# Moving the fold of row-group partial sums ahead in the first batch, and storing the last block in halves

One core of one Trainium2 chip runs the whole program. The metric is device time in microseconds (us), the median over runs; the span that a run's trace shows is some 1.8 us shorter. "Faster" or "slower" means a difference of over 2%.

## The reference, cut to what matters

```python
# x: (4, 12416, 128), inducing: (32, 128)
def mab(q, kv):
    s = scale * (q @ kv.transpose(0, 2, 1))
    a = np.exp(s - s.max(-1, keepdims=True))
    a /= a.sum(-1, keepdims=True) + 1e-09
    return a @ kv

h = mab(I, x)                 # 32 x 128 per batch: a sum over all 12416 rows
y = mab(x, h)                 # then every row of x attends to h
gate = 1 / (1 + np.exp(-(y @ w_gate)))          # 128 -> 1536
out  = (gate * (y @ w_val)) @ w_out             # 1536 -> 128
```

For the first batch, h has to be complete before anything of the large second part can begin. That stretch, from the last piece of x to the first tanh (the sigmoid is computed as a tanh), is called the head below. The part after it, the body, is the gate, value and output matmuls of all four batches. The tail is the last block's eviction and store.

## The kernel before: the parts that matter

The program is a list of named operations with their dependencies, and a recorded order of names for each engine. The order is what is played; names such as `fill8.2` are filler matmuls, eight of them here, that only keep TensorE busy.

```python
ACC = ps("acc", [P, TOK])                       # one PSUM tile for the sums of the first batch
hsum, hval = ACC[:, 288:320], ACC[:, 256:288]

def h_base():                                   # the fold: partial sums of row groups -> hval, hsum
    hev = dve(129, fin, "hev", ... tensor_copy(out=hacc, in_=ACC[:, 0 : P + 1]))
    sbc = dve(32, [hev], "hb0", ... tensor_scalar_mul(out=ssb, in0=I4, scalar1=hacc[:, P : P + 1]))
    ...                                         # "hbase": two fp32 matmuls on PE

def stage1_first(i, groups, xts):               # quad i: scores, exp, sums
    apart = i < NQ - 1                          # NQ = 6: quads 0..4 by row groups, quad 5 in place
    ...
    if apart:   # 4 row groups at once, into ACC[r:r+32, 0:129]
    else:       # in place: ones16 -> hsum, x -> hval
    fin.append(a)                               # "hv{i}.{k0}"

def h_first():
    r = dve(256, fin, "hr0", ... reciprocal(out=hden, in_=hsum))
    hTd[0] = dve(32, [r], "hc0", ... tensor_tensor(out=hT, in0=hval, in1=hden, op=ALU.mult))

def fill(o, n):
    for _ in range(n):
        PE.matmul(ACC[:, 320:512], lhsT=ident, rhs=zeros, start=False, stop=False, ...)

# last step of a unit of 4 row blocks
e = act(nt * P, ..., ACT.activation(out=os.t[:, 0:nt, :], in_=ACC[:, 0 : nt * P], func=AF.Copy, scale=0.5))
st = op("SP", ..., SP.dma_start(ov[b][:, 4 * u : 4 * u + nt, :], os.t[:, 0:nt, :]))
```

The recorded order of PE around the end of the head:

```
... hv2.0 hv3.0 fill10.1 xt4.0 ... xt5.13 s1t5.8 s1t5.0 hbase s1t5.13 hv5.8 hv5.0 hv5.13 s2t0 fo0.1 s2t2 fo0.0 sb0.2 ...
```

`xt` are transposes of x, `s1t` the scores of h, `hv` its sums, `s2t` the scores of the second attention, `fo` the folds of h into the value and gate weights.

The softmax here doesn't subtract the row's maximum and nothing guards it: scores larger than these inputs give would overflow.

## Time and profile before

| | before |
|---|---|
| time, three runs | 698.72, 699.49, 698.71 us |
| span of the profiled run | 697.2 us |
| ACT busy | 675.3 us (97%) |
| reciprocal of the sums (start) | 24.07 us |
| last cast of wv on POOL (start, length) | 24.30, 0.61 us |
| first tanh | 27.67 us |
| last eviction to end of span | 693.31 to 697.18: 3.87 us |

ACT (ScalarE) bounds the body, so only a head that ends earlier or a shorter tail can shorten the run. The prediction shows the lines.

### The profile page before, as it was taken

The numbers are of one execution on the slowest core, as the hardware profiler recorded it, in microseconds if no ns is written. First come the engines' busy times: TensorE is split into PE (matmuls) and PEld (weight loads), VectorE is DVE, ScalarE is ACT, GpSimd is POOL, SyncE is SP. The second block draws the span as 40 slices with busy tenths as digits, with TensorE's granted clock in tenths as the row PEclk, the third lists the DMA queues.
The fourth block names the chain that finished last, engine by engine and source line by source line (L and its number), as shares of the span: only waits on it lengthen the run. The fifth ranks groups of instructions, "written<-read, shape, count | busy, mean of one in ns | idle before, by whom it ended". The sixth has DMA issues, their size and how long they took to land.

```text
span 697.2 us, 20697 instructions
## 1 busy us (share of the span) xinstructions
PE 672.5 (96%) x8325; PEld 384.6 (55%) x8325; DVE 667.4 (96%) x1130; ACT 675.3 (97%) x867; POOL 435.8 (63%) x498
## 2 busy tenths in 40 slices
PE   7899999999999999999999999999999999999997
PEld 5545555555555555555555555555555555555555
DVE  4799999999999999999999999999999999999997
ACT  4899999999999999999999999999999999999995
POOL 4446756855739657766485575775674675667664
PEclk9999999999999999999999999999999999999999
DMA  9859796693655646746556559422333222242211
GB/s 352 190 127 184 162 176 157 134 184 85 146 129 135 133 109 156 149 117 140 107 123 155 122 106 140 141 71 87 88 113 109 56 85 99 63 131 89 83 48 50
DMA packets 121874, 87.72 MB, mean 126 GB/s; under 512 B 80913, under 2 KB 105009, under 8 KB 121777
## 3 DMA queue, kind: packets, MB, share of 16 engines
q1 hardware_dynamic: 117584, 76.44, 43.1%
q0 software_dynamic: 4144, 9.93, 9.2%
q8 instruction: 65, 1.06, 0.6%
q14 instruction: 33, 0.26, 0.1%
q10 hardware_dynamic: 48, 0.02, 0.0%
HBM read 39.99 MB, written 38.01 MB: 112 GB/s over the span
## 4 chain that ended last, share of the span: by engine, by line
PE 51%; ACT 26%; DVE 12%; issue 5%; DMA 3%; POOL 2%; SPq 0%; ACTq 0%; DVEq 0%; POOLq 0%
PE acc L635 26%; ACT tga L635 20%; PE v L635 17%; DVE ua L635 12%; PE g L635 8%; ACT vs L635 3%; ACT os L635 3%; DMA ua<-in_x_dram 2%; DMA xT<-in_x_dram 1%; DMA out_dram<-os 1%; POOL sm L635 0%; SPq L635 0%; POOL ua L635 0%; POOL pt L635 0%; ACT e L635 0%
## 5 line engine op out<-in xcount | busy, mean ns | idle before, releaser
L635 DVE SCALAR_TENSOR_TENSOR ua<-tga,v 128x512 f16<-128x512 f16 x1041 | 641.4, 682 | 10.6 <-PE v L635 3.0
L635 ACT ACTIVATE tga<-g 128x1024 f16<-128x1024 f32 x576 | 569.0, 1142 | 0.6 <-PE g L635 0.4
L635 PE MATMUL acc<-wo,ua 128*128 128x128 f16 x4608 | 358.8, 220 | 3.2 <-ACT os L635 0.2
L635 PEld LDWEIGHTS <-ua 128*128 128x128 f16 x4608 | 262.4, 98 | 169.2 <-issue 160.4
L635 PE MATMUL v<-a2r,hw 32*128 32x512 f16 x1200 | 322.3, 374 | 8.6 <-DVE ua L635 4.3
L635 POOL TENSOR_TENSOR pt<-tga,vs 128x512 f32<-128x512 f16 x111 | 129.1, 1163 | 171.4 <-ACT vs L635 73.6
L635 PE MATMUL g<-a2r,hw 32*128 32x512 f16 (+1 forms) x1200 | 225.7, 376 | 3.5 <-ACT tga L635 1.9
L635 PEld LDWEIGHTS <-hw 32*128 32x128 f16 x2400 | 88.7, 91 | 110.1 <-issue 44.0
L635 POOL TENSOR_TENSOR ua<-pt,vs 128x512 f16<-128x512 f32 x111 | 140.9, 1269 | 9.9 <-issue 1.2
L635 ACT COPY vs<-v 128x512 f32<-128x512 f32 x111 | 77.6, 701 | 0.2 <-PE v L635 0.2
L635 ACT ACTIVATE os<-acc 128x512 f32<-128x512 f32 (+1 forms) x99 | 68.9, 696 | 2.5 <-PE acc L635 2.4
L635 POOL TENSOR_TENSOR sm<-sm,minus 128x16 f32<-128x16 f32 (+1 forms) x21 | 63.9, 3043 | 1.6
L635 POOL TENSOR_TENSOR a2n<-e2t,sm 128x128 f16<-128x128 f16 x96 | 37.2, 482 | 1.3 <-DVE sm L635 0.4
L635 POOL DMA_DIRECT2D x<-in_x_dram x18 | 11.2, 621 | 41.5 <-ACT tga L635 40.1
L635 POOL TENSOR_TENSOR tree<-tree 128x64 f32<-128x64 f32 (+4 forms) x69 | 23.7, 343 | 5.4
L635 POOL TENSOR_TENSOR tree<-e2t 128x256 f32<-128x256 f16 (+1 forms) x23 | 15.8, 688 | 8.3 <-DMA e2t<-e 8.3
L635 ACT ACTIVATE e<-g 128x512 f16<-128x512 f32 (+1 forms) x23 | 17.0, 737 | 0.1
L635 DVE COPY xT<-g 128x1024 f16<-128x1024 f16 (+1 forms) x12 | 8.0, 666 | 8.5 <-PE g L635 8.5
L635 ACT ACTIVATE eT<-g 128x512 f16<-128x512 f32 (+1 forms) x18 | 13.0, 721 | 0.0
L635 PE MATMUL g<-ident,x 128*128 128x128 f16 x97 | 7.6, 220 | 2.7 <-ACT x L635 1.3
L635 PE MATMUL g<-xT,hT 128*32 128x512 f16 (+1 forms) x108 | 9.4, 363 | 0.0
L635 DVE SCALAR_TENSOR_TENSOR ut<-tgt,v 128x512 f16<-128x512 f16 (+1 forms) x16 | 8.7, 550 | 0.3 <-PE v L635 0.2
(83 smaller groups left out, 153.7 us busy)
## 6 DMA issues: line engine op xcount, KB each, us to landing
out_dram<-os SPq DMA_DIRECT2D x96, 256.0 KB, 2.5
a2r<-dr SPq DMA_DIRECT2D x23, 512.0 KB, 4.6
dr<-a2p SPq DMA_DIRECT2D x19, 512.0 KB, 3.5
x<-in_x_dram POOLq DMA_DIRECT2D x15, 512.0 KB, 5.6
xT<-in_x_dram SPq DMA_DIRECT2D x6, 512.0 KB, 7.4
dr<-a2p SPq DMA_DIRECT2D x4, 640.0 KB, 3.3
x<-in_x_dram POOLq DMA_DIRECT2D x3, 544.0 KB, 7.8
ua<-in_x_dram SPq DMA_DIRECT2D x3, 512.0 KB, 11.5
```

Of the source, the lines that this page charges most:

```text
L635: ins = fn(*a, **k)
```

## The change

Its intent: fold the partial sums of quads 0 to 3 while the core still waits for loads, and sum quads 4 and 5 in place, so that no fold stands between the last piece of x and h; and store the last block in two halves, so that the first half's bytes leave while the second half is evicted.

```diff
-            apart = i < NQ - 1
+            apart = i < NQ - 2
...
-    h_base()                       # after quads 0..4
+        if i == NQ - 3:            # after quads 0..3
+            h_base()
...
-        e = act(nt * P, ..., f"E{b}.{u}", ...)
-        st = op("SP", ..., SP.dma_start(ov[b][:, 4 * u : 4 * u + nt, :], os.t[:, 0:nt, :]))
+        for k in range(2 if (b, u) == (B - 1, NB - 1) else 1):
+            lo, hi = ...           # two blocks each for the last unit
+            e = act((hi - lo) * P, ..., f"E{x}{b}.{u}", ...)
+            q, n = (ACT, "ACT") if k else (SP, "SP")
+            st = op(n, ..., q.dma_start(ov[b][:, 4 * u + lo : 4 * u + hi, :], os.t[:, lo:hi, :]))
```

The recorded orders were made anew. The pieces that count:

```diff
 PE
-  ... hv2.0 hv3.0 fill10.1 xt4.0 ... xt5.13 s1t5.8 s1t5.0 hbase s1t5.13 hv5.8 hv5.0 hv5.13 s2t0 fo0.1 s2t2 fo0.0 sb0.2
+  ... s1t4.0 fill8.1 xt4.8 hbase xt5.0 ... s1t5.13 hv5.0 hv5.8 hv5.13 fill8.2 s2t0 s2t2 fo0.1 fo0.0 fill3.7 sb0.2
 ACT
-  ... xs2t0 fc0.1 xs2t2 fc0.0 ...             ... E3.22 E3.24 E3.23
+  ... xs2t0 xs2t2 fc0.1 fc0.0 ...             ... E3.22 E3.24 E3.23 Eh3.23 sth3.23
```

## The prediction

> **What bounds the kernel now.** I read the page first (busy time of the engines), then the busy time by stretches, then the timeline of the first 30 us and of the last 14 us, because the change touches only those two ends.
>
> ```profile
> PE 672.5 (96%) x8325; PEld 384.6 (55%) x8325; DVE 667.4 (96%) x1130; ACT 675.3 (97%) x867; POOL 435.8 (63%) x498
> ...
> 5.00:10.00 5.00, 4.10 (x58) 2.81 (x57) 2.15 (x4) 2.65 (x4) 2.03 (x3) 1.00 1.03 418
> 15.00:20.00 5.00, 4.11 (x95) 3.48 (x92) 2.07 (x3) 2.80 (x6) 2.01 (x4) 1.00 1.03 401
> 25.00:30.00 5.00, 4.88 (x108) 2.59 (x105) 4.32 (x14) 4.98 (x10) 0.56 (x1) 1.00 0.58 88
> ```
>
> The last three lines are stretches; their columns are the length, then busy time of PE, its weight loads, DVE, ACT and POOL, the clock, the DMA share and GB/s. Until 20 us the loads run at 400 to 418 GB/s with a DMA share of 1.03 and every engine has gaps: the prologue is bound by the loads of x. From 25 us ACT is full. Summed over the five stretches of 0 to 25 us ACT is busy 12.2 us, over 680 to 697.2 us 9.1 us; so from 25 to 680 us it is busy 675.3 - 21.3 = 654.0 of 655 us. The body is ACT's, without slack. Whatever makes ACT begin its unbroken run earlier is kept to the end, and nothing else before 25 us counts.
>
> So the head is the way from the last piece of x (landed by 20.2 us) to the first tanh at 27.67 us. The timeline, cut to what matters (start, length, engine, operation):
>
> ```profile
> 20.16 0.29 DVE L635 CAST x<-ua 128x256 f16<-128x256 f32 x1 [0.35 <-DMA ua<-in_x_dram]
> ...
> 21.54 0.29 DVE L635 COPY hacc<-acc 128x129 f32<-128x129 f32 x1 [0.48 <-PE acc L635]
> 21.95 0.58 DVE L635 TENSOR_SCALAR ssb<-I,hacc 128x32 f32<-128x32 f32 x1
> 22.45 0.41 DVE L635 COPY xT<-g 128x512 f16<-128x512 f16 x1
> 22.59 0.41 PE L635 MATMUL acc<-ssb,ones 128*128 128x32 f32 x2
> 24.07 0.36 DVE L635 RECIPROCAL hden<-acc 128x32 f32<-128x32 f32 x1 [1.21 <-PE acc L635]
> 24.30 0.61 POOL L635 CAST wv<-tga 128x512 f16<-128x512 f32 x1
> 24.46 0.19 DVE L635 TENSOR_TENSOR hT<-acc,hden 128x32 f16<-128x32 f32 x1
> 24.97 0.29 PE L635 MATMUL g<-wv,hT 128*32 128x256 f16 x2
> 25.30 0.37 ACT L635 CAST hw<-g 128x256 f16<-128x256 f32 x1
> 26.19 0.41 PE L635 MATMUL v<-ident,nb 128*32 128x128 f16 x16
> ```
>
> The fold of the partial sums (copy of the accumulator, scaled identity, two pairs of fp32 matmuls) stands between the last transposes and h: the scaled identity holds DVE up to 22.45, when the last xT copy starts, and the ssb matmuls hold PE up to 22.92. h comes out at 24.46 + 0.19 = 24.65. Note the POOL line: the last weight cast ends at 24.91, and the first fold matmul on wv starts at 24.97. The weights are ready only just after h.
>
> The tail is one path with no overlap:
>
> ```profile
> 693.31 0.60 ACT L635 ACTIVATE os<-acc 128x512 f32<-128x512 f32 x1 [2.42 <-PE acc L635]
> 693.93 0.33 SPq L635 DMA_DIRECT2D out_dram<-os  x1
> ...
> 694.70:694.80 0.10, 0.00 (x0) 0.00 (x0) 0.00 (x0) 0.00 (x0) 0.00 (x0) 1.00 0.39 143
> 695.40:695.50 0.10, 0.00 (x0) 0.00 (x0) 0.00 (x0) 0.00 (x0) 0.00 (x0) 0.50 0.51 185
> ```
>
> Bytes flow from about 694.75 to 695.5, 0.8 us after the issue; then come the receipt and the closing waits, to 697.2.
>
> **What the skill says.** The Trainium skill, "DMA: Bandwidth & Descriptors", section "Anatomy of one DMA", gives about 2.0 us fixed plus bytes over 436 GB/s, most of the fixed part being the receipt after the last byte (fitted there on the GpSimd path). The trace half agrees: stores of 256 KB land in 2.2 us at the end, about 0.75 us of it data. Halving a transfer saves only data time. Its section "Issuing engines are not separate DMA queues" says a second issuing engine saves only issue time: the same here, the two halves share 16 DMA engines. "Perfetto Trace Analysis", section "Optimizing Scalar/DVE Operations", gives every ScalarE operation a fixed access overhead: the trace has 0.60 us for 128x512 and 0.37 us for 128x256 from PSUM, so 0.14 fixed and 0.23 per 256 columns. "TensorEngine Tiling (Array Packing)", "Key Properties", says that a change of tiling mode drains the array; quad 4 loses two such changes, too small for me to see in the timeline.
>
> **The change part by part.**
>
> *Fold earlier.* Quads 0 to 3 still accumulate by row groups; their fold now comes behind the ninth xT copy (the first of quad 4), in time in which DVE and PE wait for loads (DVE busy 2.07 of 5 us in 15 to 20). It is the same work: copy 0.29, scaling 0.58, PE about 0.7. Quad 4 is now summed in place: for each group of 8 blocks 16 matmuls, 0.40 us (23.29 to 23.69 for such a group), where 8 by row groups took 0.30: +0.2 us on PE for both groups. I walked the new PE order with these durations: xt4.8 at 18.7, fold matmuls to 19.85, xt5.0 and xt5.8 to 20.6, s1t4.8 and hv4.0 to 21.25, xt5.13 to 21.5, then s1t5.0, s1t5.8, hv4.8, s1t5.13, and the three last sums to about 23.4. The reciprocal then starts near 23.5 instead of 24.07: h comes about 0.55 us earlier (an estimate from these rows).
>
> *What of it is kept.* Not 0.55. Loads and POOL's order are untouched, so the last weight cast still ends near 24.91 and the fold on wv still starts at 24.97; the copy hw at 25.30 does not move, nor does the score matmul behind it, which needs the PSUM buffer that this copy frees at 25.67 (it starts at 25.72). What moves: the second row group (s2t2) goes ahead of the fold, so its 0.35 us on ACT falls into idle time. And nb is ready at about 25.6 instead of 26.13, so the transposes at 26.19 can start when the score matmul lets them, at about 25.95. From there the path to the first gate matmul is as before (copy 26.65 becomes 26.41, ends 26.83, gate 27.24 becomes 27.00). ACT: 25.30 + 0.29 + 0.49 + 0.49 + 0.27 + 0.49 = 27.32, plus some 0.1 of gaps. Both say first tanh at 27.42 to 27.43 against 27.67: a gain of **0.24 us**, which ACT carries through the body. The order of the body is the same except for the renumbered fills.
>
> *Halves of the last store.* Both halves wait for the last matmul (the second has no wait of its own). First half: 693.31 + 0.37, issued by SP near 693.70, 0.23 earlier. Second: starts 0.27 later, ends 693.95 (0.04 later than the whole one), issued by ACT. It moves 128 KB, 0.4 us less of data, the first half being nearly through by then. 0.40 - 0.04 - about 0.08 for the issue on ACT (0.42 us there at the start of the kernel against 0.33 on SP) = **0.28 us**.
>
> Sum: 0.24 + 0.28 = 0.52; 698.72 - 0.52 = **698.2 us**.
>
> **Rivals.** (a) The weights do not bind and h's whole 0.55 us is kept: for it, wg is cast well ahead and only wv's second part is late; against it, 24.91 and 24.97 in the trace and an unchanged POOL order. Time: 697.9. (b) The head gives nothing, because ACT's work from 25.30 on is packed and the new order of PE (16 more matmuls in quad 4, xt5.13 behind hv4.0) takes the slack back: 698.45. (c) The second half's store costs as much as it saves, since ACT's queue has issued nothing since the first microsecond and two receipts must now arrive: tail 0, time 698.5. (d) A different phase makes the body collect waits, say on PSUM buffers: ACT idles only about 1 us in 655 now, so a new order of arrivals can only lose; 0.5 us lost would return the time to 698.7.
>
> **Range and chances.** The runs of before spread from 698.71 to 699.49, as much as the whole gain. Rivals (a) with a full tail and (b) with (c) span 697.9 to 698.7; with the run-to-run spread I take 697.3 to 699.0. Two per cent are 14 us, and both ends together hold under 12 us beyond the loads: the verdict "same" is nearly certain.
>
> **What would show it.** Right: hacc and ssb before 19 us; reciprocal of hden near 23.5; the wv fold and hw still at 24.97 and 25.30; eb 128x256 before hw; first tanh near 27.4; ACT full from there; two os of 128x256 at the end, stores from SP and ACT, bytes over by about 695.2 less the head's gain. Wrong: a wv cast that ends elsewhere than 24.9; a first tanh at 27.1 (rival a) or 27.6 (b); a last byte no earlier after the last matmul than 2.2 us (c); ACT idle in the body up by more than 0.2 us (d).

## The result, and the profile after

Runs of the changed kernel: 699.25, 699.29, 699.46, 700.42 us, median 699.38; of the kernel before on the same chip: 698.71, 698.72, 699.39, 699.49, median 699.06. A ratio here is the mean time of one kernel's fast runs over that of the other's fast runs of the same rounds, so it is not quite the ratio of those medians: 1.0008, with a 95% interval of 0.999 to 1.0025. The time, 699.38, lies above the predicted range (697.3 to 699.0). Where 0.5 us were to be won, none was.

The page's busy line first (busy time, share of the span, number of instructions):

```profile
PE 675.1 (97%) x8350; PEld 386.9 (55%) x8350; DVE 666.7 (95%) x1130; ACT 675.5 (97%) x868; POOL 435.8 (62%) x498
```

PE has 25 more matmuls. Sixteen come from quad 4, summed in place (two per block of rows instead of one); the other nine can only be fillers. Next, two of the stretches that were shown of before, with the same columns:

```profile
15.00:20.00 5.00, 4.63 (x117) 4.04 (x114) 2.95 (x6) 3.78 (x10) 2.33 (x4) 1.00 1.03 401
...
25.00:30.00 5.00, 4.33 (x71) 2.11 (x69) 3.26 (x12) 3.06 (x8) 0.56 (x1) 0.67 0.31 39
```

Before 20 us DVE and ACT do more, as planned. From 25 to 30 us ACT is busy 3.06 of 5 us where it was full before, and the granted clock is 0.67. The timeline of the changed kernel's head (start, length, engine, operation, idle time before it and what ended it):

```profile
17.74 0.28 DVE L636 COPY hacc<-acc 128x129 f32<-128x129 f32 x1
...
18.15 0.24 DVE L636 TENSOR_SCALAR ssb<-I,hacc 128x32 f32<-128x32 f32 x1
...
22.90 0.25 PE L636 MATMUL acc<-ae,x 128*128 128x32 f16 x4
23.00 0.33 PE L636 MATMUL acc<-zeros,ident 128*128 128x192 f16 x2
24.23 0.61 POOL L636 CAST wv<-tga 128x512 f16<-128x512 f32 x1
24.43 0.66 PE L636 MATMUL acc<-zeros,ident 128*128 128x192 f16 x6 [1.10 <-issue]
25.12 0.36 DVE L636 RECIPROCAL hden<-acc 128x32 f32<-128x32 f32 x1 [3.25 <-PE acc L636]
25.51 0.19 DVE L636 TENSOR_TENSOR hT<-acc,hden 128x32 f16<-128x32 f32 x1
...
29.75 7.44 ACT L636 ACTIVATE tga<-g 128x1024 f16<-128x1024 f32 x8 [0.20 <-PE g L636]
```

The fold is early (17.74 and 18.15, both before 19 us as predicted), and the sums are done at 23.15 instead of 24.05. But the reciprocal starts at 25.12, not near 23.5. It waits for `acc`, and what still writes `acc` are eight filler matmuls, in front of which PE even stood idle for 1.10 us with nothing awaited. The first tanh starts at 29.75, which is 2.08 us later than before. The tail, as timeline and bytes (last two columns of the short stretches: DMA share and GB/s):

```profile
695.00 0.66 ACT L636 ACTIVATE os<-acc 128x256 f32<-128x256 f32 x2 [2.42 <-PE acc L636]
695.69 0.38 ACTq L636 DMA_DIRECT2D out_dram<-os  x1
```

```profile
696.20:696.30 0.10, 0.00 (x0) 0.00 (x0) 0.00 (x0) 0.00 (x0) 0.00 (x0) 1.00 0.40 133
...
696.90:697.00 0.10, 0.00 (x0) 0.00 (x0) 0.00 (x0) 0.00 (x0) 0.00 (x0) 1.00 0.89 297
```

From the start of the last eviction (695.00) to the end of the span (698.64) it is 3.64 us, against 3.87. That part works. So do the steps of the fold. The profiled run (700.42) was the slowest of its four, and part of its 2.08 us is bad luck, as the experiments show; but something in the head takes back more than the change gives.

### The profile page after: what moved, and what is told of

It reads as the page before. It is cut to its first block, busy times and chain, and to the rows that moved or that the text cites. A ratio compares the mean times of both kernels' runs of the same rounds, so it can differ in the third digit from the quotient of the medians.

```text
span 698.6 us, 20751 instructions
## 1 busy us (share of the span) xinstructions
PE 675.1 (97%) x8350; PEld 386.9 (55%) x8350; DVE 666.7 (95%) x1130; ACT 675.5 (97%) x868; POOL 435.8 (62%) x498
## 4 chain that ended last, share of the span: by engine, by line
PE 55%; ACT 27%; DVE 11%; issue 5%; POOL 1%; DMA 1%; SPq 0%; ACTq 0%; DVEq 0%
PE acc L636 27%; ACT tga L636 20%; PE v L636 18%; DVE ua L636 10%; PE g L636 9%; ACT os L636 3%; ACT vs L636 3%; DMA xT<-in_x_dram 1%; POOL sm L636 0%; ACT tgt L636 0%; ACT e L636 0%; POOL a2n L636 0%; DVE xT L636 0%; POOL ua L636 0%; POOL pt L636 0%
## 5 line engine op out<-in xcount | busy, mean ns | idle before, releaser
L636 ACT ACTIVATE os<-acc 128x512 f32<-128x512 f32 (+2 forms) x100 | 69.0, 691 | 2.5 <-PE acc L636 2.4
L636 ACT ACTIVATE ae<-v 128x256 f16<-128x256 f32 (+2 forms) x13 | 4.6, 369 | 8.0 <-PE v L636 7.2
L636 PE MATMUL acc<-zeros,ident 128*128 128x192 f16 x55 | 9.2, 253 | 1.1 <-issue 1.1
```

The costliest lines, as they stand in the source:

```text
L636: ins = fn(*a, **k)
```

## The experiments

**How they are read.** The arrival of the loads shifts by up to 0.4 us from run to run (the first wv cast on POOL starts at 22.46 us in e2, at 22.86 in e10), so head times are counted from the start of that cast, called w below. And the granted clock differs from run to run: stretches of 3.4 us at half clock appear in some runs. In the kept traces a run with a mean clock of 0.999 or 1.000 has none before its last matmul; I call it whole, and compare the means of whole runs of the same job where tenths of a microsecond matter. In brackets is how many runs were whole.

The theory after the result, called the filler theory here: the eight fillers ahead of the second stage (`fill8.2`) write the tile of the sums, so the reciprocal waits for them, and h comes later by their duration and by whatever idle time PE has among them. The built programs say the same: the count of PE's instructions that the reciprocal awaits is that of the last sum in the kernel before (666), and that of the last filler in the changed one (710; its last sum is 694), though the fillers write columns 320 to 511 of the tile and the reciprocal reads 288 to 319. Dependencies are kept by tile here, not by column. Rivals: P, the in-place sums themselves are the cost; K, the clock, which fillers may keep whole; and the prediction's own d, waits in the body.

| kernel | w to reciprocal | w to first tanh | first tanh to last eviction | tail | median us | mean of whole runs | before, whole, same job |
|---|---|---|---|---|---|---|---|
| before | 1.31 | 4.91 | 665.64 | 3.87 | 699.06 | clocks not listed | |
| after | 2.59 | 7.22 | 665.25 | 3.64 | 699.38 | 699.27 (2 of 4) | clocks not listed |
| e0 after again | 2.15 | 5.75 | 665.70 | 3.65 | 699.07 | 698.99 (4 of 6) | 698.72 (4 of 11) |
| e1 no fillers there | 0.49 | 6.14 | 665.19 | 3.65 | 699.13 | 698.75 (2 of 6) | 698.72 |
| e2 halves only | 1.31 | 4.91 | 665.18 | 3.65 | 700.49 | 698.11 (2 of 6) | 698.72 |
| e4 other fillers dropped | 1.18 | 4.78 | 665.60 | 3.65 | 698.63 | 698.62 (4 of 6) | 698.72 |
| e3 head only | 2.07 | 5.66 | 665.77 | 3.87 | 699.99 | 699.63 (1 of 6) | 698.75 (9 of 11) |
| e5 before plus fillers | 1.98 | 5.58 | 665.19 | 3.89 | 699.28 | 699.29 (6 of 6) | 698.75 |
| e6 fillers, other tile | 0.50 | 4.70 | 665.76 | 3.65 | 698.77 | 698.65 (4 of 6) | 698.75 |
| e7 as e6, fewer fillers | 0.50 | 4.80 | 665.72 | 3.64 | 698.79 | 698.83 (4 of 6) | 698.75 |
| e8 as e6, x load later | 0.51 | 4.86 | 666.65 | 3.65 | 699.39 | 699.30 (4 of 6) | 698.79 (5 of 11) |
| e9 halves plus fillers | 1.32 | 4.92 | 665.54 | 3.64 | 698.66 | 698.57 (6 of 6) | 698.79 |
| e10 e2 again | 1.34 | 4.93 | 665.35 | 3.66 | 698.61 | 698.53 (4 of 6) | 698.79 |

The middle columns are of one profiled run each. Those of after, e0, e1 and e4 were not whole: a half-clock stretch lay between 9 and 15 us in after, e0 and e4, and one in the head in after and e1. Of the times put on record before the runs, those for e1, e3, e4, e6, e7 and e8 were missed: the means of the whole runs came out 0.15 to 0.80 us above the ranges; the body (below) is part of it. Every kernel gave the right result, and every verdict was "same" at 2%.

**e0_after_again**: the changed kernel, unedited.

> The changed kernel once more, unedited. Theory (F): the eight filler matmuls put between the last sum and s2t0 write the same PSUM tile as the sums, so the reciprocal of hden waits for the last filler; and an idle of PE of about 1.1 us with nothing awaited falls inside them. Then this profile again has the reciprocal at about 25.1 us (25.12 in the first profile, 24.07 in the kernel before) and PE idle from about 23.3 to 24.4, also when the clock is whole. Rival (C): the loss is the clock that dropped to half at 10 and at 27 us in the one profile; then a profile with a clock of 0.999 or more has the reciprocal near 23.5 and the first tanh near 27.4. Time: F 699.3 with a whole clock, ratio to before 1.000 to 1.002.

Measured: median 699.07, ratio 0.9997 (0.9983 to 1.0011). The late reciprocal is there again (2.15 after w, before 1.31), but not the 1.10 us of idle time in front of the fillers: here about a quarter of that; its last sum ended later (1.18 after w, 0.62 in the first profile). So there are a fixed part, the fillers, and a part that changes from run to run.

**e1_no_fill82**: the filler theory by itself, with these eight taken out.

```diff
- hv5.13 fill8.2 s2t0
+ hv5.13 s2t0
```

> The changed kernel without the eight fillers between the last sum and s2t0; nothing else. F: reciprocal at about 23.2 us; the 1.1 us idle of PE, if it belongs to a place in the instruction stream (instruction 700 of PE), now falls in the middle of s2t0 and ends again near 24.4, so h is no longer late but s2t0 is only 0.2 us earlier than before the change; first tanh at 27.4 to 27.6 (27.67 before), tail as in the changed kernel: 698.0 to 698.4, ratio to before 0.999 to 0.9995. C: as the changed kernel, 699.3. Rival (P): the new order of PE and the in-place sums of quad 4 are what costs; then the last sum ends later than 24.0 and the time stays at 699.3.

Measured: the reciprocal starts 0.49 us after w, 1.66 earlier than in e0. That is what the filler theory asked for, and it takes P down: the in-place sums are all there, and h comes out early. But the first tanh of the profiled run was late (6.14) for another reason: a stretch of half clock from 24.8 to 28.2 us, right in the head. The median is 699.13, and only 2 of 6 runs were whole; their mean, 698.75, is above the 698.0 to 698.4 expected.

**e2_halves_only**: the kernel before with the split of the last store alone (the loop over `k` of the change, and `Eh3.23 sth3.23` at the end of ACT's order).

> The kernel before with the last block's store in halves, nothing else. My step: from the start of the last os copy to the end of the span 3.60 us instead of 3.89 (read from the two profiles), so 0.29 us less, ratio 0.9996; head as before (reciprocal 24.07, first tanh 27.67). Rival: the second queue's completion costs the gain back, 3.9 us and ratio 1.0000.

Measured: tail 3.65 against 3.87, the head as before. The two whole runs were 698.25 and 697.97; the others at lower clocks, up to 706.41. The median, 700.49, says nothing of the change.

**e4_no_fill81**: the other group of fillers dropped, the one far ahead of the last sums.

```diff
- s1t4.0 fill8.1 xt4.8 hbase
+ s1t4.0 xt4.8 hbase
```

> The changed kernel without the earlier eight fillers (those behind s1t4.0), the later eight kept. All later PE instructions move 16 places forward, so the fillers in front of the reciprocal end at instruction 694, ahead of place 700. If the 1.1 us idle belongs to place 700 of the instruction stream: the fillers run without a gap, reciprocal at about 23.7 (0.65 late for the fillers alone), the idle moves into s2t0 and ends near 24.4, first tanh 27.4 to 27.6, time 698.0 to 698.4. If it belongs to the fillers or to the moment (23.3 us): the idle stays among the fillers, reciprocal near 25.1, time 699.3. A third way: fewer fillers leave PE idle and its clock drops near 20 us; then a clock under 0.998 in the profile.

Measured: the eight fillers ahead of `s2t0` took 0.82 us with no gap, the reciprocal started at 1.18 and the first tanh at 4.78. Median 698.63. Dropping fillers elsewhere took away the idle time among these ones. PE's instruction at which it had stood idle, number 700 of its stream, now lies behind them.

**e5_before_plus_fill**: the suspected cost alone, put into the kernel before.

```diff
- hv5.13 s2t0
+ hv5.13 fill8.99 s2t0
```

> The kernel before with eight fillers added between its last sum and s2t0, the same place as in the changed kernel; nothing else. F: the reciprocal waits for them, 1.31 + 0.66 = about 1.97 after the first wv cast, and the first tanh goes from 4.91 to 5.4 to 5.6; whole-clock runs at 699.1 to 699.3 against 698.48 to 698.68 of the kernel before. New theory (K): fillers there keep the clock whole in more of the runs; so far 8 of 12 runs with these fillers had a clock of 1.0, 4 of 23 without. K expects 3 or more of 6 here with clock 1.0; without K, 1 of 6. Rival (W, the weights bind anyway, a late reciprocal costs nothing): first tanh at 4.9.

Its timeline:

```profile
23.93 0.82 PE L635 MATMUL acc<-zeros,ident 128*128 128x192 f16 x8
...
24.79 0.36 DVE L635 RECIPROCAL hden<-acc 128x32 f32<-128x32 f32 x1 [1.88 <-PE acc L635]
...
28.39 9.38 ACT L635 ACTIVATE tga<-g 128x1024 f16<-128x1024 f32 x10
```

Eight fillers of 0.82 us, and the reciprocal starts just as they end (24.75 to 24.79), though the last sum is long done. Against before, the reciprocal moves by 1.98 - 1.31 = 0.67 us and the first tanh by 5.58 - 4.91 = 0.67 us. In whole runs the time moves by 699.29 - 698.75 = 0.54 us. All six runs were whole.

**e3_head_only**: the change without its tail (the old single eviction and store).

> The changed kernel with the store of before (whole); only the head's part of the change. The loads land up to 0.3 us apart from run to run, so times in the head are counted from the start of the first wv cast on GpSimd. So far, first tanh after that cast: before 4.91, halves only 4.91, changed 7.22 and 5.75 (two profiles), without the early fillers 4.78. F: reciprocal 2.1 to 2.6 after the cast (before 1.31), first tanh 5.6 or later at a whole clock; runs with clock 1.0 at 699.0 to 699.3, that is 0.2 to 0.3 above the changed kernel's whole-clock runs (698.85 to 699.08), since the tail's 0.23 is missing. Rival (P, the sums in place cost): last sum later than 24.05.

Measured: tail 3.87, first tanh 5.66 after w, that is 0.75 later than before; PE idle for 0.69 us among the fillers. Its one whole run took 699.63, 0.88 above the whole runs of before. The head part of the change, with its fillers as they stand, is a loss.

**e6_fill_other_tile**: the decisive one. All instructions stay where they are; the eight fillers only write another PSUM tile.

```diff
 def fill(o, n):
     for _ in range(n):
+        if o.name == "fill8.2":
+            PE.matmul(PSUM["G"][1][:, 320:512], lhsT=ident, rhs=zeros, start=True, stop=True, ...)
+            continue
         PE.matmul(ACC[:, 320:512], lhsT=ident, rhs=zeros, start=False, stop=False, ...)
```

> The changed kernel; the eight fillers in front of s2t0 write to a PSUM tile that is idle there instead of the tile of the sums. Count, place and order of all instructions are the same. F: the reciprocal no longer waits for them: 0.5 to 0.7 after the first wv cast (2.15 and 2.59 in the changed kernel); s2t0 follows the fillers, with the idle at place 700 still among them, 1.7 to 1.9 after the cast (before: 1.95); the last wv cast binds from there, first tanh 4.7 to 4.8; whole-clock runs 698.1 to 698.5, below the changed kernel's 698.85 to 699.08. K: clock 1.0 in about 4 of 6. If the wait is not by tile: as the changed kernel, reciprocal at 2.1 or more.

Its timeline:

```profile
23.13 0.32 PE L636 MATMUL g<-zeros,ident 128*128 128x192 f16 x2
23.32 0.36 DVE L636 RECIPROCAL hden<-acc 128x32 f32<-128x32 f32 x1 [1.30 <-PE acc L636]
...
24.36 0.62 POOL L636 CAST wv<-tga 128x512 f16<-128x512 f32 x1
25.04 0.29 PE L636 MATMUL g<-wv,hT 128*32 128x256 f16 x2 [0.22 <-POOL wv L636]
...
25.36 0.86 ACT L636 CAST hw<-g 128x256 f16<-128x256 f32 x2 [0.34 <-PE g L636]
...
27.52 8.36 ACT L636 ACTIVATE tga<-g 128x1024 f16<-128x1024 f32 x9
```

The reciprocal starts at 23.32, while the fillers run (the prediction had 23.5). The fold on wv then waits for POOL's last cast, as the prediction said, and the first tanh comes 4.70 after w, 0.21 earlier than before (predicted: 0.24). The filler theory is shown: the same instructions, another tile, and the head gains what it was to gain (the reciprocal awaits instruction 694 again, the last sum).

But the time does not. The whole runs average 698.65, only 0.10 under those of before, where head and tail should give 0.21 + 0.22 = 0.43.

**e7_fill_other_no81**: e6 and e4 together.

> As the one before, and without the earlier eight fillers, so that the idle at place 700 falls behind these fillers. F: reciprocal 0.4 to 0.6 after the first wv cast, fillers without a gap (0.82 for eight), s2t0 1.2 to 1.7 after it, but the first tanh no earlier than 4.6, since the fold still waits for the last wv cast: 698.1 to 698.5, as the one before within 0.2. If the weights do not bind: first tanh at 4.2 to 4.4 and 697.8.

Measured: as e6 (0.50, 4.80, median 698.79). The second stage starts 0.18 earlier, and the first tanh does not: further room in the head is worth nothing, because the cast of wv ends 2.25 after w (2.16 in e6). Counted from the end of that cast, the first tanh comes 2.54 to 2.55 us later in e6, e7 and e8, and 2.76 us later in the kernel before: the head's 0.21 us is there in all three.

**e8_late_x**: where did the head's gain go? ACT has one wait in its first 20 us of tanh, near 36 us. In chains: the transposes of the first exponentials (e2t) are DMA work, POOL's tree waits for them, DVE and PE for POOL, ACT for PE. The lines of the kernel before, from POOL's and ACT's timelines:

```profile
26.23 0.56 POOL L635 DMA_DIRECT2D x<-in_x_dram  x1 [1.31 <-issue]
32.24 0.67 POOL L635 TENSOR_TENSOR tree<-e2t 128x256 f32<-128x256 f16 x1 [5.46 <-DMA e2t<-e]
```

```profile
36.19 2.86 ACT L635 ACTIVATE tga<-g 128x1024 f16<-128x1024 f32 x3 [0.16 <-PE g L635]
```

And of e6:

```profile
26.30 0.56 POOL L636 DMA_DIRECT2D x<-in_x_dram  x1 [1.31 <-issue]
32.33 0.67 POOL L636 TENSOR_TENSOR tree<-e2t 128x256 f32<-128x256 f16 x1 [5.47 <-DMA e2t<-e]
```

```profile
36.28 2.87 ACT L636 ACTIVATE tga<-g 128x1024 f16<-128x1024 f32 x3 [0.41 <-PE g L636]
```

From the issue of the next batch's x load (512 KB) to the tree it is 6.01 us before and 6.03 in e6 (5.84 to 6.19 in all profiles but that of e8), however early the first tanh is. The wait follows the tree: in the nine profiles in which the tree begins 4.40 us or more after the first tanh, ACT's idle time near 36 us is that distance less 4.40 us, within 0.03 (0.16 us for 4.57 before, 0.36 for 4.77 in e0, 0.41 for 4.81 in e6, 0.43 for 4.85 in e3). It is not the early tanh alone that makes it: e0 and e3 have a late one, and wait as long as e6. The edit moves that load behind the tree, and what uses it later to match:

```diff
 POOL
- ... wv.1 ld1.0 tr0.1 mu0.1
+ ... wv.1 tr0.1 ld1.0 mu0.1
 SP
- et0.1 et0.2 xd1.0.2 xd1.0.3 bt0.1 xd1.0.0 xd1.0.1 wr0.1 re0.1
+ et0.1 et0.2 bt0.1 wr0.1 xd1.0.2 xd1.0.3 re0.1 xd1.0.0 xd1.0.1
 PE, ACT
  sa1.0 and xsa1.0 three or four gate blocks later
```

> e6_fill_other_tile with the first load of the second batch's x moved behind the first sum tree on GpSimd (and the four transposes of it and the matmul that uses them moved later to match). It asks where the head's gain of e6 went. Theory: in every profile the tree on the transposed exponentials begins 5.8 to 6.1 us after that 512 KB load is issued, whatever the first tanh did, because the transposes and the load share the DMA engines (DMA share 0.9 to 1.3 from 27 to 32 us); so with an earlier tanh ACT waits 0.3 to 0.4 us for PE near 36 us. With the load away: tree begins at most 4.2 us after the first tanh (e6: 4.81), no ACT wait over 0.1 us between 30 and 45 us, whole-clock time 698.2 to 698.5 (e6: 698.65). Rival: the wait comes from DVE's or PE's own order; tree may come earlier but the ACT wait stays at 0.3 to 0.4 us and the time at 698.6 to 698.8. Risk: the moved transposes come late near 49 us and ACT waits there instead; then the time is 698.6 or more with the wait near 50 us.

POOL's and ACT's timelines of e8:

```profile
30.16 0.67 POOL L635 TENSOR_TENSOR tree<-e2t 128x256 f32<-128x256 f16 x1 [5.34 <-DMA e2t<-e]
32.66 0.59 POOL L635 DMA_DIRECT2D x<-in_x_dram  x1 [0.29 <-issue]
```

```profile
50.73 1.94 ACT L635 ACTIVATE tga<-g 128x1024 f16<-128x1024 f32 x2 [0.15 <-POOL ua L635]
53.23 0.60 ACT L635 ACTIVATE eT<-g 128x512 f16<-128x512 f32 x1 [0.57 <-PE g L635]
```

The tree comes 2.78 us after the first tanh (e6: 4.81), and ACT waits for nothing from its first tanh to 50 us. So the load did hold the transposes up, and through them ACT. (The transposes of x that moved along with it are issued in e6 at 31.82 us, only 0.51 us before the tree, so they are not what held it up.) But x is now late for the next batch, ACT waits 0.15 + 0.57 us near 50 us (and 0.25 at 79.8), and the time is worse: 699.30 in whole runs against 698.79. That was the risk, and it came true. The cause of the wait is shown; a cure is not.

**e9_halves_plus_fill** and **e10_halves_again**: is the clock a matter of these fillers? e9 is the halves-only kernel with five fillers behind the last sum, into the other tile (`hv5.13 fill5.99 s2t0`, and the edit of e6); e10 is e2 unchanged, for comparison.

> The kernel before with the last store in halves, and five filler matmuls behind the last sum that write another PSUM tile, so that nothing waits for their tile. Reciprocal 1.3 us after the first wv cast as before, first tanh at 4.9 to 5.05, tail 3.65. Theory K (fillers in front of the second stage keep the clock whole): at least 5 of 6 runs at a clock of 0.999 or more, and whole-clock runs at 698.3 to 698.6. Rival (the clock is chance and not of these fillers): about as many whole runs as for e10_halves_again and the kernel before of the same job.

> e2_halves_only once more, unchanged. First: tail 3.65 (before 3.87), whole-clock runs 0.2 to 0.5 us under those of the kernel before, as in the first run of it. Second, for theory K: without the fillers at most half of the runs at a clock of 0.999 or more (e2: 2 of 6); the rival expects a share no different from that of e9_halves_plus_fill.

Measured: tails of 3.64 and 3.66. Whole runs: 698.57 (6 of 6) and 698.53 (4 of 6), against 698.79 (5 of 11) of before: a gain of 0.22 and 0.26 us, the size of the tail's. On the clock: the kernel before with fillers added at that place (e5, e9) was whole in 12 of 12 runs, without them (before in the three experiment jobs, e2, e10) in 18 + 6 = 24 of 45. But that share differs by job: in those of e5 and e9 the kernels without these fillers were whole in 9 of 11 and in 9 of 17 runs, and e10 with 4 of 6 missed the "at most half" that K expected. Against K stand the kernels with the changed head too, whole in 23 of 40 runs with the fillers in place (1 of 6 in e3). For K, then: suggested in the kernel before, not settled.

What comes before a half-clock stretch can be read as well, but it gives no rule. In the changed kernel's profile the trace has one from 26.71 to 30.12 us. About the time before it and the stretch itself (columns as above):

```profile
23.50:26.90 3.40, 1.80 (x29) 1.18 (x28) 1.03 (x5) 0.85 (x4) 1.24 (x3) 0.97 0.75 76
26.90:30.30 3.40, 3.40 (x51) 1.53 (x49) 2.23 (x8) 2.51 (x5) 0.56 (x1) 0.53 0.47 65
```

And the same time in e6, whose clock stayed whole:

```profile
23.50:26.90 3.40, 3.03 (x57) 1.86 (x56) 2.06 (x9) 2.07 (x6) 2.04 (x4) 1.00 0.89 92
```

In e1, the time before its half-clock stretch, and a piece of the stretch:

```profile
21.50:25.00 3.50, 2.42 (x77) 2.13 (x74) 1.39 (x6) 1.44 (x5) 3.10 (x4) 0.97 1.23 169
25.00:25.50 0.50, 0.41 (x6) 0.13 (x5) 0.50 (x2) 0.00 (x0) 0.04 (x1) 0.50 0.75 92
```

In the changed kernel PE was busy 1.80 of 3.40 us, then came 3.4 us at half clock; with 3.03 of 3.40 in e6 it did not come. But PE's busy share does not decide it: in e1 the stretch came after 2.42 of 3.50 us, and in the same run the 3.41 us from 7.75 us on, with 1.94 busy, were followed by a whole clock. Nor does it take a late h: in e1 the reciprocal was early. In the changed kernel's profile the stretch went along with a further loss of about 1 us from the reciprocal to the tanh: 7.22 - 2.59 = 4.63 us against 5.75 - 2.15 = 3.60 in e0. That the late reciprocal brought the stretch on is not shown.

The Trainium skill, "TensorE: Matmul & The Clock Gate", section "What's actually happening", says that the clock is halved after an idle window of about 3.4 us of a free-running counter. The length agrees (3.41 us each time), and a free-running counter would fit the chance from run to run; but none of the windows before a half-clock stretch was idle: PE was busy for 1.63 to 2.52 of the 3.41 us (after, e0, e1, e4).

## Why the prediction was wrong

- *Fold earlier*: right. hacc at 17.74, ssb at 18.15, the last sum at 23.15 (predicted about 23.4), and with the fillers out of the way the reciprocal at 23.32 (predicted 23.5).
- *"The order of the body is the same except for the renumbered fills"*: here it failed. I took all fillers for renumbered old ones and for harmless. Eight of them were new at the one place where nothing may be added: behind the last sum, writing the tile that the reciprocal reads. The step "the reciprocal then starts near 23.5" had no term for them. The eight fillers take 0.82 us: put into the kernel before, they cost 0.67 us to the reciprocal and to the first tanh (e5); in the change they eat up what the early sums win (reciprocal 1.18 after w in e4, where PE did not stand idle among them; 0.49 to 0.51 where nothing waits for them or they are gone; 1.31 before). The rest is PE's idle time among them, which holds h up only because the reciprocal waits for the last of them, and in e0 a later last sum: the reciprocal came 0.84 us (e0) to 1.28 us (the profiled run) later than before, not 0.55 earlier. The recorded order named the eight fillers in plain sight, and the wait follows from their tile; the idle time could not be read from either.
- *What of it is kept* (0.24; the sum for ACT comes to 27.33, not 27.32, which changes nothing): right in mechanism and size once the fillers write elsewhere: 0.21 (e6; in e7 and e8 too, counted from the last wv cast). Rival a is out: the last wv cast binds (PE waited for it 0.22 us in e6). Rival b is not the story either: the head can gain.
- *Halves of the last store* (0.28): right; 0.22 us, from 3.87 to 3.65 in every profile with the halves, and 0.22 to 0.26 us in the whole runs of e9 and e10. Rival c is out.
- *Rival d*, body waits, which I let stand at 0.5 us but did not put into the sum: true. The wait near 36 us is 0.41 us in e6, against 0.16 before, since the transposes land at a time set by the load of x and not by the tanh (shown by e8). One profile of each is not enough for the size: the old order's wait is 0 to 0.16 us in before, e2, e5, e9 and e10. The table's body column gives it better: from the first tanh to the last eviction those five take 665.18 to 665.64 us (mean 665.38), while e0, e3, e4, e6 and e7, which have the new order and no half-clock stretch after w, take 665.60 to 665.77 (mean 665.71). So some 0.33 of the 0.43 us that head and tail win in e6 is given back, which leaves about the 0.10 that whole runs measured; that it fits so closely is partly luck, with 0.46 us between the five old-order profiles.

The sum of the measured terms is a range, since the idle time differs from run to run: to the first tanh 0.13 won (e4, none among the fillers) to 0.84 lost (e0), body about 0.33 lost, tail 0.22 won; together 0.02 won to 0.95 lost. Whole runs of the changed kernel lost 0.27 (e0, against those of its job) and about 0.5 (699.27 in the first comparison, against the 698.72 to 698.79 of before in the three experiment jobs), and the profiled run of e0, which was not whole, 0.87 (699.59 - 698.72).

Not fully closed: what PE's idle time with nothing awaited is (1.10, 0.69, 0.25, 0.19 and 0.75 us among the same fillers in after, e3, e0, e6 and e8; none in e4, e5; 0.36 in e7, where it falls into s2t0). The kept traces say more than the runs asked. It stands in front of the same instruction of PE's stream, and in all six profiles that instruction starts 1.36 to 1.44 us after a 16 KB transfer has ended on the DMA queue that the page lists as q8, "instruction": 23.02 and 24.43 us in the profiled run of the change, 22.26 and 23.65 us in e6. The end of that transfer wanders, from 0.56 us before w (e6) to 0.49 us after it (after), and the idle time with it. So it fits a late fetch of instructions; no run moved the fetch, so this is not shown by experiment. Nor is it settled how far fillers govern the clock.

No version beats the kernel before by more than 0.04% in whole runs, apart from two whole runs of e2 that e10 did not repeat. The halves alone, with fillers that nothing waits for (e9), gave the steadiest times: 698.32 to 698.71.

## What to carry to other kernels

A filler instruction is free only if nobody waits for what it writes: give it a tile of its own. When a change brings a new recorded order, list what is new between the last producer and the first consumer on the critical path before estimating anything else. And a gain ahead of a saturated engine is kept only up to the next event whose time it does not move, here first a weight cast, then the transposes behind a load.

## What the Trainium skill lacked or had wrong

- "TensorE: Matmul & The Clock Gate": the clock was halved for 3.41 us after a window in which PE was busy 1.80 of 3.40 us, so the window need not be idle. With 3.03 of 3.40 us it stayed whole. Neither is a rule: in e1 it was halved after 2.42 of 3.50 us, and not after 1.94 of 3.41 us.
- "Runtime: NRT & Kernel Launch", section "Instruction fetch mechanics", says that PE's instructions are fetched in blocks of 256 by a DMA queue of their own, and calls the cost mostly hidden. If the idle time above is such a fetch, as its steady distance of 1.36 to 1.44 us from the end of a transfer on an instruction queue suggests (six profiles), it was not hidden here: up to 1.10 us, and different from run to run. No run moved the fetch.
- No page that I read gives what a 512 KB load costs DMA transposes issued just behind it: the transposes' reader started 4.81 us after the first tanh with the load, 2.78 us without (e6, e8).
